# Seven products of quarters for both layers of the last batch in an attention and mixer kernel

## The chip, the cores and the metric

The kernel runs on one core of one Trainium2 chip. A core has five engines with a program each: TensorE (PE in the profile, with its weight loads as PEld), VectorE (DVE), ScalarE (ACT), GpSimd (POOL) and SyncE (SP), which here only starts DMAs. TensorE multiplies a stationary block[...] with a moving block and accumulates into PSUM; VectorE and ScalarE read PSUM and SBUF[...]. The metric is the device time of the whole kernel in microseconds (us); lower is better. Three runs of the kernel before gave 1704.02, 1704.91 and 1705.40 us, median 1704.91.

## The reference

Top-k attention over 8 batches and 8 heads (576 rows, head width 64, the 32 largest scores of a row kept), whose output goes as x (8 x 576 x 512) through a mixer:

```
xt = x.transpose(0, 2, 1)
h = xt @ U @ V
u = x + h.transpose(0, 2, 1)
ch = np.maximum(u @ w_ch1, 0.0) @ w_ch2
return (u + ch).astype(np.float32)
```

The two layers of the last but one line are what the change is about: u (576 x 512) times w_ch1 (512 x 2048), everything negative set to zero, times w_ch2 (2048 x 512), for each batch. All of it is in fp32.

## The kernel before

The attention runs in steps of 128 rows of a pair of heads. For each step VectorE looks for the 32 largest scores, GpSimd and ScalarE make mask and exponential, TensorE multiplies by the values. When the four pairs of heads of a batch are done, `mixed` (line 630) has written u, turned, into the tile uT: its 512 channels lie on 4 blocks of 128 partitions, its 576 rows along the columns.

The two layers of a batch are a generator, `mlp` (line 692), put into the list `fillers` by the last `mixed` of the batch. `fill` (line 793) takes matmuls from it in small portions between the steps of the next batch, so that TensorE has work while VectorE searches. The last batch has no next batch: its generator is emptied by the loop at the end of the kernel. The program order of each engine is the order in which this code emits instructions; nothing reorders it later.

`mlp` takes the columns of uT in two spans, 320 and 256 wide (`SPAN`). In each span:

- layer one: for each of the 16 blocks of 128 hidden channels, 4 matmuls (line 701) with a block of w1 as stationary and a block of uT as moving operand, summed in one PSUM buffer `mm` of two; ScalarE writes its positive part into hT (line 714);
- layer two: for each of the 4 blocks of output channels, 16 matmuls (line 719) with w2 and hT; then u is added (in the last batch by VectorE, line 731, in the others by ScalarE and GpSimd, lines 733 and 734).

One matmul of the code is two records in the profile, since fp32 goes through the array in two instructions.

`turned_back` (line 737) brings a result to row order. It is put off by `later(12, ...)` until 12 more matmuls have been emitted (`tick`). In most batches TensorE transposes it into PSUM (line 764), ScalarE copies it (line 766) and one or two DMAs of SP write it out (line 770). In the last batch VectorE transposes in blocks of 32 x 32 instead (line 746), and 8 or 12 DMAs with short rows put the blocks in place (lines 751 and 756); only the very last result goes by TensorE. The tile `ob`, from which these DMAs read, has two buffers, and so has the result tile `oT`.

w1 is one tile of 128 x 4 x 2048, w2 one of 128 x 16 x 512. The PSUM buffers are three pools of two: `sc` (scores), `tp` (transposes and small products) and `mm` (the two layers).

Of the kernel before, what the change touches and what calls it, by code (L numbers as in the profile page):

```python
# [8 lines left out]
F32 = mybir.dt.float32  # L9
U8 = mybir.dt.uint8  # L10
U32 = mybir.dt.uint32
AF = mybir.ActivationFunctionType
ALU = mybir.AluOpType

TOPK = 32
# [11 lines left out]
def kernel(  # L27
# [28 lines left out]
    nc = tc.nc  # L56
    B, H, S, D = q.shape
    P = 128
    C = H * D
    R = moe_U.shape[1] // 2  # L60
    F = moe_w_ch1.shape[1] // 2
    NF, NC = F // P, C // P
    NT, TAIL = 4, 64
    MAIN = NT * P
    HALF = S // 2
# [10 lines left out]
    BLK = 32  # L76
    HT = 8
# [3 lines left out]
    const = ctx.enter_context(tc.tile_pool(name="const", bufs=1))  # L81
    loads = ctx.enter_context(tc.tile_pool(name="loads", bufs=1))
    attn = ctx.enter_context(tc.tile_pool(name="attn", bufs=2))
    small = ctx.enter_context(tc.tile_pool(name="small", bufs=8))
    mlpp = ctx.enter_context(tc.tile_pool(name="mlpp", bufs=2))
# [8 lines left out]
    OFF = {0: 0, 1: P, NT: 2 * P, 2: 2 * P + TAIL, 3: 3 * P + TAIL}  # L94
# [15 lines left out]
        nc.gpsimd.memset(vts[i], 0.0)  # L110
    for x in xs:
        nc.gpsimd.memset(x[:, NT, :], 0.0)
    w1 = const.tile([P, NC, F], F32, name="w1")
    w2 = const.tile([P, NF, C], F32, name="w2")
    U = const.tile([P, NT + 1, R], F32, name="U")

# [9 lines left out]
    def rows(t):  # L126
        return P if t < NT else TAIL
# [74 lines left out]
    for f in range(0, F, SLAB):  # L202
        for cc in range(NC):
            params.append(
                ([moe_w_ch1[cc * P:(cc + 1) * P, 2 * f:2 * (f + SLAB)]], w1[:, cc, f:f + SLAB])
            )
    for c in range(0, C, P):
        for f in range(0, NF, NT):
# [421 lines left out]
    def mixed(g, wait, lag=0):  # L630

        for _ in range(lag):
            yield
        b, gi = divmod(g, NPAIR)
        if gi == 0:
            uTs[b] = mlpp.tile([P, NC, S], F32, tag="uT", name="uT")
        XT, den = XTs.pop(g), dens[g]
        X = xs[g % 2]
        tp = ps_t.tile([P, NT, P], F32, tag="tp", name="tp")
        for t in range(NT):  # L640
            nc.tensor.transpose(tp[:, t, :], XT[:, cols(t)], ident)  # L641
        X4 = X[:, 0:NT, :].rearrange("p t (h d) -> p t h d", h=2)
        tp4 = tp.rearrange("p t (h d) -> p t h d", h=2)
        den4 = den[:, 0 : 2 * NT].rearrange("p (t h) -> p t h ()", h=2).to_broadcast([P, NT, 2, D])
        nc.scalar.copy(X4, tp4)
        nc.gpsimd.tensor_tensor(X4, X4, den4, ALU.mult)
        for _ in range(wait):
            yield
        pT = ps_t.tile([P, P], F32, tag="tp", name="pT")
        for t in range(NT + 1):  # L650
            i = t % NT * R
            nc.tensor.matmul(  # L652
                pT[i : i + R, :],
                lhsT=U[:, t, :],
                rhs=X[:, t, :],
                start=(t < NT),
                stop=(0 < t),
            )
        Tb = mlpp.tile([P, P], F32, tag="Tb", name="Tb")
        nc.scalar.copy(Tb, pT)  # L660
        yield
        for chunks, (lo, hi) in zip(PARTS, SPAN):
            up = ps_t.tile([P, WIDE], F32, tag="tp", name="up")
            nc.tensor.matmul(up[:, 0 : hi - lo], lhsT=Tb, rhs=V[:, lo:hi], start=True, stop=False)  # L664
            for t in chunks:
                nc.tensor.matmul(  # L666
                    up[:, OFF[t] - lo : OFF[t] - lo + rows(t)],
                    lhsT=X[:, t, :],
                    rhs=ident if t < NT else ident2,
                    is_transpose=True if t < NT else None,  # L670
                    start=False,
                    stop=(t == chunks[-1]),
                )
            nc.scalar.copy(uTs[b][:, gi, lo:hi], up[:, 0 : hi - lo])
            yield
        if gi == NPAIR - 1:
            fillers.append(mlp(b))

    posts, ticks = [], 0

    def later(wait, job):

        posts.append((ticks + wait, job))

    def tick():

        nonlocal ticks
        ticks += 1
        if posts and posts[0][0] <= ticks:
            posts.pop(0)[1]()  # L690

    def mlp(b):

        uT = uTs.pop(b)
        for chunks, (lo, hi) in zip(PARTS, SPAN):
            w = hi - lo
            hTs = []
            for f in range(NF):
                ph = ps_m.tile([P, C], F32, tag="mm", name="mm")
                for cc in range(NC):  # L700
                    nc.tensor.matmul(  # L701
                        ph[:, 0:w],
                        lhsT=w1[:, cc, f * P : (f + 1) * P],
                        rhs=uT[:, cc, lo:hi],
                        start=(cc == 0),
                        stop=(cc == NC - 1),
                    )
                    tick()
                    if cc < NC - 1:
                        yield w / C  # L710
                if f % 2 == 0:
                    hT = mlpp.tile([P, 2, WIDE], F32, tag="hT", name="hT", bufs=HT)
                    hTs += [hT[:, 0], hT[:, 1]]
                nc.scalar.activation(hTs[f][:, 0:w], ph[:, 0:w], AF.Relu)  # L714
                yield w / C
            for c in range(NC):
                po = ps_m.tile([P, C], F32, tag="mm", name="mm")
                for f in range(NF):
                    nc.tensor.matmul(  # L719
                        po[:, 0:w],  # L720
                        lhsT=w2[:, f, c * P : (c + 1) * P],
                        rhs=hTs[f][:, 0:w],
                        start=(f == 0),
                        stop=(f == NF - 1),
                    )
                    tick()
                    if f < NF - 1:
                        yield w / C
                oT = mlpp.tile([P, WIDE], F32, tag="oT", name="oT")
                if b == B - 1:  # L730
                    nc.vector.tensor_tensor(oT[:, 0:w], uT[:, c, lo:hi], po[:, 0:w], ALU.add)  # L731
                else:
                    nc.scalar.copy(oT[:, 0:w], po[:, 0:w])
                    nc.gpsimd.tensor_tensor(oT[:, 0:w], oT[:, 0:w], uT[:, c, lo:hi], ALU.add)
                later(12, turned_back(b, chunks, lo, c, oT))
                yield w / C
    def turned_back(b, chunks, lo, c, oT):


        def run():  # L740
            cs = slice(c * P, (c + 1) * P)
            if b == B - 1 and (lo, c) != (SPAN[1][0], NC - 1):

                w = sum(rows(t) for t in chunks)
                ob = mlpp.tile([P, 3 * P], F32, tag="ob", name="ob", bufs=2)
                nc.vector.transpose(ob[:, 0:w], oT[:, 0:w])
                for a in range(4):
                    cs = slice(c * P + a * BLK, c * P + (a + 1) * BLK)
                    ba = ob[a * BLK : (a + 1) * BLK]
                    for t in chunks[0:2]:  # L750
                        nc.sync.dma_start(
                            out[b, 0:MAIN, cs].rearrange("(m i t) c -> t i m c", i=BLK, t=NT)[t],
                            ba[:, OFF[t] - lo : OFF[t] - lo + P].rearrange("i (m c) -> i m c", c=BLK),
                        )
                    if NT in chunks:
                        nc.sync.dma_start(
                            out[b, MAIN:S, cs].rearrange("(m i) c -> i m c", i=BLK),
                            ba[:, 2 * P : 2 * P + TAIL].rearrange("i (m c) -> i m c", c=BLK),
                        )
                return  # L760
            tp = ps_t.tile([P, 3, P], F32, tag="tp", name="tp")
            for i, t in enumerate(chunks):
                n = rows(t)
                nc.tensor.transpose(tp[0:n, i, :], oT[:, OFF[t] - lo : OFF[t] - lo + n], ident)  # L764
            ob = mlpp.tile([P, 3, P], F32, tag="ob", name="ob", bufs=2)
            nc.scalar.copy(ob[:, 0:2], tp[:, 0:2, :])
            if NT in chunks:
                nc.scalar.copy(ob[0:TAIL, 2], tp[0:TAIL, 2, :])
            t = chunks[0]
            nc.sync.dma_start(  # L770
                out[b, 0:MAIN, cs].rearrange("(p t) c -> p t c", t=NT)[:, t : t + 2, :],
                ob[:, 0:2],
            )
            if NT in chunks:
                nc.sync.dma_start(out[b, MAIN:S, cs], ob[0:TAIL, 2])

        return run

    MLP_WORK = 2 * NF * NC * S / C

# [230 lines left out]
```

## Time and profile before

| | |
|---|---|
| median of three runs | 1704.91 us |
| the profiled execution | 1704.56 us |
| its span, first to last instruction | 1702.7 us |
| mean granted TensorE clock | 0.97 |
| TensorE busy | 1606.2 us, 94% |
| VectorE busy | 1495.9 us, 88% |
| ScalarE busy | 993.5 us, 58% |
| GpSimd busy | 900.5 us, 53% |
| chain that ended last | TensorE 85%, VectorE 12% |

A busy share is an average over the span. A line of the chain gives the share of the span that a line of code holds on the path that ended last: 29% each for the matmuls of line 719 and of line 701. A group line gives line, engine, operation, output and input tiles and shapes, the count, then busy time and the mean of one in ns, then the idle time of the engine just before and what ended it.

From 1574.16 us on, TensorE works on the two layers of the last batch, and from 1580.84 us on nothing else is left of the batches before:

| window, us | TensorE | VectorE | ScalarE | GpSimd |
|---|---|---|---|---|
| 1500 to 1510 | 10.00 | 10.00 | 7.69 | 5.79 |
| 1560 to 1570 | 10.00 | 0.00 | 1.81 | 1.72 |
| 1600 to 1650 | 50.00 | 4.00 | 3.35 | 0.00 |
| 1650 to 1690 | 40.00 | 1.73 | 5.00 | 0.00 |

### The profile page before, as it was taken

The page shows a single profiled execution, that of the slowest core. Times are in us where ns is not written, and L with a number is a line of the kernel's source. Part 1 is how long each engine was busy: PE and PEld are TensorE (multiplying, and loading weights), DVE is VectorE, ACT ScalarE, POOL GpSimd, SP SyncE. Part 2 cuts the span into 40 slices and gives each one's busy share as a digit, 9 for nine tenths or more (in the row PEclk, how much of TensorE's full clock was granted, in tenths as well). Part 3 has the DMA queues.
Part 4 walks back from the last instruction along what each step waited for, and adds up shares of the span by engine and source line. Part 5 has one row for each costly group of instructions (what it writes and reads, how often), then busy time and mean ns, then how long its engine had stood idle before and what let it go on. Part 6 is the DMA issues. An engine that isn't in the chain of part 4 may idle for free.

```text
span 1702.7 us, 29005 instructions
## 1 busy us (share of the span) xinstructions
PE 1606.2 (94%) x9385; PEld 1210.6 (71%) x9385; DVE 1495.9 (88%) x4286; ACT 993.5 (58%) x2422; POOL 900.5 (53%) x695
## 2 busy tenths in 40 slices
PE   4566789999999999999999999999999999999999
PEld 2444556787677877788777877788777877788777
DVE  7999998999999999999999999999999999991000
ACT  4888778665556656565656556565656556563100
POOL 4778568656555555555555555555555555551000
PEclk7788899999999999999999999999999999999999
DMA  3322232255445454554544454554544454532010
GB/s 87 96 83 85 65 85 69 63 135 129 124 122 128 118 134 119 140 127 118 124 123 125 122 130 119 137 127 122 125 122 124 120 135 117 134 106 79 4 16 13
DMA packets 275832, 180.95 MB, mean 106 GB/s; under 512 B 173920, under 2 KB 260192, under 8 KB 275680
## 3 DMA queue, kind: packets, MB, share of 16 engines
q1 hardware_dynamic: 259648, 117.49, 29.8%
q10 hardware_dynamic: 16032, 61.61, 11.3%
q8 instruction: 74, 1.21, 0.3%
q14 instruction: 78, 0.64, 0.1%
HBM read 108.23 MB, written 70.78 MB: 105 GB/s over the span
## 4 chain that ended last, share of the span: by engine, by line
PE 85%; DVE 12%; ACT 1%; POOL 1%; issue 1%; DMA 0%; SPq 0%; DVEq 0%; POOLq 0%; ACTq 0%
PE mm L719 29%; PE mm L701 29%; PE sc L334 9%; PE O L618 7%; DVE m L485 5%; DVE upper L480 5%; PE up L664 2%; PE O L602 2%; DVE first L467 2%; PE O L615 1%; PE tp L577 1%; PE up L666 1%; PE pT L652 1%; PE tp L764 1%; PE tp L641 1%; DVE w L186 1%
## 5 line engine op out<-in xcount | busy, mean ns | idle before, releaser
L719 PE MATMUL mm<-hT,w 128*128 128x256 f32 (+1 forms) x2048 | 530.4, 409 | 0.0
L701 PE MATMUL mm<-uT,w 128*128 128x256 f32 (+1 forms) x2048 | 529.6, 410 | 0.0
L515 POOL TENSOR_TENSOR Ssb<-Ssb,E 128x576 f32<-128x576 f32 x243 | 339.7, 1417 | 275.7 <-ACT E L514 275.4
L701 PEld LDWEIGHTS mm<-uT,w 128*128 128x128 f32 x2048 | 379.2, 191 | 109.5 <-issue 8.4
L719 PEld LDWEIGHTS mm<-hT,w 128*128 128x128 f32 x2048 | 377.2, 190 | 104.4 <-issue 12.7
L485 DVE MAX8 m<-upper 128x8 f32<-128x304 f32 (+1 forms) x780 | 367.2, 512 | 0.7
L480 DVE MATCH_REPLACE8 upper<-m,upper 128x304 f32<-128x304 f32 (+1 forms) x520 | 259.7, 507 | 0.0
L397 POOL TENSOR_TENSOR lower<-Ssb 128x576 uint32<-128x576 uint32 x108 | 152.7, 1414 | 152.8 <-issue 100.1
L334 PE MATMUL sc<-qkT 64*128 64x288 f32 (+1 forms) x1334 | 210.2, 437 | 11.2 <-ACT Ssb L367 7.8
L404 ACT ACTIVATE Ssb<-Ssb,nmax 128x576 f32<-128x576 f32 x258 | 200.9, 780 | 18.6 <-POOL Ssb L491 9.7
L714 ACT ACTIVATE hT<-mm 128x320 f32<-128x320 f32 (+1 forms) x256 | 104.6, 409 | 181.9 <-PE mm L701 178.2
L400 POOL TENSOR_TENSOR lower<-lower,upper 128x576 uint32<-128x576 uint32 x108 | 152.7, 1414 | 100.3 <-DVE upper L399 95.2
L452 DVE MAX8 upper<-lower 128x8 f32<-128x288 f32 x432 | 172.3, 440 | 9.8 <-POOL lower L400 9.7
L514 ACT ACTIVATE E<-Ssb,least 128x576 f32<-128x576 f32 x243 | 176.2, 768 | 4.3
L334 PEld LDWEIGHTS sc<-qkT 64*128 64x128 f32 (+1 forms) x1334 | 115.6, 182 | 73.7 <-issue 29.0
L541 DVE STREAM_TRANSPOSE y<-Ssb 128x512 f32<-128x512 f32 (+1 forms) x312 | 154.8, 546 | 7.0 <-ACT Ssb L404 6.4
L360 ACT COPY Ssb<-sc 128x576 f32<-128x576 f32 x216 | 127.7, 644 | 36.6 <-PE sc L334 36.6
L618 PE MATMUL O<-PT,va 128*64 128x128 f32 x2048 | 144.5, 285 | 0.0
L731 DVE TENSOR_TENSOR oT<-uT,mm 128x320 f32<-128x320 f32 (+1 forms) x8 | 3.6, 454 | 144.6 <-PE mm L719 144.6
L618 PEld LDWEIGHTS O<-PT,va 128*64 128x64 f32 x2048 | 113.1, 140 | 16.1 <-issue 1.3
L399 DVE TENSOR_TENSOR upper<-sc,Ssb 128x576 f32<-128x576 f32 x108 | 80.3, 744 | 22.2 <-ACT Ssb L360 22.0
L480 DVE MATCH_REPLACE8 upper<-first,upper 128x304 f32<-128x304 f32 x216 | 97.7, 460 | 0.0
(111 smaller groups left out, 1893.3 us busy)
## 6 DMA issues: line engine op xcount, KB each, us to landing
away<-y SPq DMA_DIRECT2D x416, 144.0 KB, 2.5
PT<-away ACTq DMA_DIRECT2D x104, 576.0 KB, 3.8
raw<-in_moe_w_ch_dram SPq DMA_DIRECT2D x32, 512.0 KB, 3.8
va<-in_v_dram SPq DMA_DIRECT2D x64, 128.0 KB, 2.3
out_dram<-ob SPq DMA_DIRECT2D x57, 128.0 KB, 2.0
ld<-in_q_dram SPq DMA_DIRECT2D x108, 64.0 KB, 2.7
ld<-in_k_dram SPq DMA_DIRECT2D x108, 64.0 KB, 2.5
ld<-in_q_dram SPq DMA_DIRECT2D x108, 8.0 KB, 3.0
```

The costliest lines, as they stand in the source:

```text
L334: nc.tensor.matmul(out, lhsT=qkT[half(h), 0, cols(t)], rhs=qkT[half(h), 1, lo:hi], start=True, stop=True,)
L397: nc.gpsimd.tensor_tensor(bottom, a.bitcast(U32), b.bitcast(U32), ALU.add)
L404: nc.scalar.activation(E, chunk, AF.Exp, bias=nmax, scale=SCALE, accum_out=total)
L452: nc.vector.max(spot, lower)
L480: nc.vector.match_replace(nxt, ms[c], curs[c], NEG)
L485: nc.vector.max(ms[c], curs[c])
L514: nc.scalar.activation(gap, chunk, AF.Relu, bias=least[:, c : c + 1], scale=-WIDEN)
L515: nc.gpsimd.tensor_tensor(chunk, chunk, gap, ALU.subtract)
L541: nc.vector.transpose(y[:, :, i * NT : i * NT + c].rearrange("p r c j -> p c r j"), E2[:, a : a + c * P].rearrange("p (c r j) -> p c r j", ...
L618: nc.tensor.matmul(O[half(h)], lhsT=va[:, h, j, :], rhs=PT[:, NT * h + j], start=False, stop=(j == NT - 1),)
L701: nc.tensor.matmul(ph[:, 0:w], lhsT=w1[:, cc, f * P : (f + 1) * P], rhs=uT[:, cc, lo:hi], start=(cc == 0), stop=(cc == NC - 1),)
L719: nc.tensor.matmul(po[:, 0:w], lhsT=w2[:, f, c * P : (c + 1) * P], rhs=hTs[f][:, 0:w], start=(f == 0), stop=(f == NF - 1),)
```

## The change

The last batch goes through a new generator, `closing`, in place of `mlp`. It cuts the stationary matrix A, the moving matrix B and the result C of each layer into quarters and computes the four quarters of C with seven products instead of eight:

```
S1 = A21+A22   S2 = S1-A11    S3 = A11-A21   S4 = A12-S2
T1 = B12-B11   T2 = B22-T1    T3 = B22-B12   T4 = B21-T2
P1 = A11 B11   P5 = S1 T1     P6 = S2 T2     P7 = S3 T3
U2 = P1+P6     U3 = U2+P7
C11 = P1 + A12 B21     C12 = U2 + P5 + S4 B22
C21 = U3 + A22 T4      C22 = U3 + P5
```

The columns are cut into 288 and 288. Layer one goes in 8 rounds, each for one block of hidden channels of the lower and one of the upper half, with 2 matmuls in a product; layer two in 2 rounds with 8 matmuls in a product. x, y and z are three accumulators in three pools of PSUM: x collects C11, y collects P5 and then C12, z collects P6, P7 and the last product of C21; P1, P5, U2 and U3 are read from them in between, while the matmuls of other accumulators run. The last product of a round's z (`held`) is put off until two products of the next round have been emitted. The weight sums of layer one are made by GpSimd two rounds ahead, those of layer two by VectorE, into the space of w1, which is cut into four tiles for that (`w1s`). The differences of layer one's results are made by VectorE (`turned_sums`). The results of layer one lie in the tiles that the attention no longer needs. In `give`, all four results of the first round of layer two and the first of the second go by VectorE's transpose and 12 DMAs each; the last three go by TensorE's transpose, put off by 5 matmuls.

```
-    w1 = const.tile([P, NC, F], F32, name="w1")
+    W1Q = F // NT
+    w1s = [const.tile([P, NC, W1Q], F32, name=f"w1{i}") for i in range(NT)]
...
-            fillers.append(mlp(b))
+            fillers.append(closing(b) if b == B - 1 else mlp(b))
...
+    def closing(b):
...
+        def sums(engine, a11, a12, a21, a22, s1, s2, s3, s4):
+            engine.tensor_tensor(s1, a21, a22, add)
+            engine.tensor_tensor(s3, a11, a21, sub)
+            engine.tensor_tensor(s2, s1, a11, sub)
+            engine.tensor_tensor(s4, a12, s2, sub)
...
+        nc.vector.tensor_tensor(t1, b12, b11, sub)
+        nc.vector.tensor_tensor(t2, b22, t1, sub)
+        nc.vector.tensor_tensor(t3, b22, b12, sub)
+        nc.vector.tensor_tensor(t4, b21, t2, sub)
...
+        def first_sums(j):
+            raw_ = mlpp.tile([P, 2 * C], U32, tag="raw", name="raw", bufs=3)
...
+            sums(nc.gpsimd, *weights(j), *blocks_)
...
+        sets = {0: first_sums(0), 1: first_sums(1)}
...
+            def turned_sums(j):
+                h11, h12, h21, h22, x1, x2, x4 = halves[j]
+                nc.vector.tensor_tensor(x1, h12, h11, sub)
+                nc.vector.tensor_tensor(h12, h22, h12, sub)
+                nc.vector.tensor_tensor(x2, h22, x1, sub)
+                nc.vector.tensor_tensor(x4, h21, x2, sub)
...
+            def fourth(j, z, p1, a22):
+                yield from product(z, a22, t4, False)
+                h21 = halves[j][2]
+                nc.vector.tensor_tensor(h21, z, p1, add)
+                nc.scalar.activation(h21, h21, AF.Relu)
...
+            for j in range(KF):
...
+                x = ps_s.tile([P, 2, 512], F32, tag="sc", name="sc")[:, 0, 0:HALF]
+                y = ps_t.tile([P, C], F32, tag="tp", name="tp")[:, 0:HALF]
+                z = ps_m.tile([P, C], F32, tag="mm", name="mm")[:, 0:HALF]
+                p1, p5, u2, u3 = temporaries()
+                yield from product(x, a11, b11)
+                nc.scalar.copy(p1, x)
+                yield from product(y, s1, t1)
+                nc.scalar.copy(p5, y)
+                if held:
+                    nc.scalar.activation(halves[j - 1][3], halves[j - 1][3], AF.Relu)
+                    yield from held
+                if j + 2 < KF:
+                    sets[j + 2] = first_sums(j + 2)
+                yield from product(z, s2, t2)
+                nc.vector.tensor_tensor(u2, z, p1, add)
+                if ahead:
+                    ahead.pop(0)()
+                yield from product(x, a12, b21, False)
+                nc.scalar.activation(h11, x, AF.Relu)
+                yield from product(y, s4, b22, False)
+                nc.vector.tensor_tensor(h12, u2, y, add)
+                nc.scalar.activation(h12, h12, AF.Relu)
+                yield from product(z, s3, t3, False)
+                nc.vector.tensor_tensor(u3, z, p1, add)
+                nc.gpsimd.tensor_tensor(h22, u3, p5, add)
+                if j > 0:
+                    turned_sums(j - 1)
+                held = fourth(j, z, p1, a22)
+                if j == KF // 2:
+                    ahead = s_of(0)
...
+            for m in range(KC):
...
+                yield from product(x, a11, h11s)
+                p1u = attn.tile([P, MAIN], F32, tag="XT", name="XT", bufs=1)[:, 0:HALF]
+                nc.scalar.copy(p1, x)
+                nc.gpsimd.tensor_tensor(p1u, p1, u21, add)
+                if held:
+                    nc.scalar.activation(halves[-1][3], halves[-1][3], AF.Relu)
+                    yield from held
+                    held = None
+                    turned_sums(KF - 1)
+                    ahead = s_of(1)
+                yield from product(y, s1, t1s)
+                nc.scalar.copy(p5, y)
+                nc.gpsimd.tensor_tensor(p5, p5, u22, add)
+                yield from product(z, s2, t2s)
+                nc.vector.tensor_tensor(u2, z, p1, add)
+                nc.gpsimd.tensor_tensor(u2, u2, u12, add)
+                yield from product(x, a12, h21s, False)
+                give(b, m, 0, x, u11, m == 0 or None)
+                yield from product(z, s3, t3s, False)
+                nc.vector.tensor_tensor(u3, z, p1, add)
+                give(b, m + KC, 1, u3, p5, m == 0)
+                yield from product(y, s4, h22s, False)
+                give(b, m, 1, y, u2, m == 0)
+                while ahead:
+                    ahead.pop(0)()
+                yield from product(z, a22, t4s, False)
+                give(b, m + KC, 0, z, p1u, m == 0)
...
+    def give(b, c, n, part, rest, blocks_=True):
+
+        oT = mlpp.tile([P, WIDE], F32, tag="oT", name="oT")
+        nc.vector.tensor_tensor(oT[:, 0:HALF], part, rest, ALU.add)
...
+        if blocks_ is not False:
+            ob = mlpp.tile([P, 3 * P], F32, tag="ob", name="ob", bufs=2)
+            nc.vector.transpose(ob[:, 0:HALF], oT[:, 0:HALF])
+            for a in range(4):
...
+            return
+
+        def run():
+            tp = ps_t.tile([P, 3, P], F32, tag="tp", name="tp")
+            for i in range(2):
+                nc.tensor.transpose(tp[:, i, :], oT[:, at_ + i * P : at_ + (i + 1) * P], ident)
+            nc.tensor.transpose(tp[0:BLK, 2, :], oT[:, tail_at : tail_at + BLK], ident)
+            ob = mlpp.tile([P, 3, P], F32, tag="ob", name="ob", bufs=2)
+            nc.scalar.copy(ob[:, 0:2], tp[:, 0:2, :])
+            nc.scalar.copy(ob[0:BLK, 2], tp[0:BLK, 2, :])
...
+        later(5, run)
```

`s_of(m)` lists the four weight sums of layer two's round m (VectorE, 1024 elements each). `mlp` and `turned_back` lose their branches for the last batch.

## The prediction

> **What bounds the kernel now.** I read the page's slices first, then the chain of waits after 1573 us, then the groups by shape. The slices (tenths of busy time in 40 slices; the last row is the granted TensorE clock):
>
> ```profile
> PE   4566789999999999999999999999999999999999
> ...
> DVE  7999998999999999999999999999999999991000
> ...
> POOL 4778568656555555555555555555555555551000
> PEclk7788899999999999999999999999999999999999
> ```
>
> In the last three slices TensorE is full at full clock and VectorE and GpSimd have almost nothing to do. The chain in order of time (start, length, what) says what fills them:
>
> ```profile
> 1574.16 6.46 PE mm L701 x24
> 1580.62 0.22 PE tp L764 x2
> 1580.84 28.00 PE mm L701 x104
> 1608.84 34.45 PE mm L719 x128
> 1643.29 27.63 PE mm L701 x128
> 1670.92 27.64 PE mm L719 x128
> ...
> 1698.58 0.43 DVE oT L731
> ...
> 1699.06 0.45 PE tp L764 x2
> ```
>
> This is the last batch, alone: 512 records (two for each matmul in the code), 124.18 us, 0.22 us of transposes, not one wait. The span ends 4.14 us after the last matmul (1702.70 - 1698.56). So here every matmul removed is time removed, as long as TensorE isn't made to wait.
>
> **What one record costs.** 320 columns: 34.45 / 128 = 0.2691 us; 256 columns: 27.64 / 128 = 0.2159 us; that is 0.83 ns a column. 288 columns, halfway: 0.2425 us. A busy neighbourhood doesn't change this: 24 records of 256 columns at 1507.89 us took 5.18 us (0.2158 each) while VectorE was busy 10.00 of 10 us and GpSimd 5.79.
>
> **What the change removes and adds on TensorE.** Ahead of the last batch the order on all engines stays as it was. Then, per layer, 7 products of quarters in place of 8: layer one 8 rounds x 7 x 2 matmuls, layer two 2 rounds x 7 x 8, together 224 matmuls or 448 records of 288 columns: 448 x 0.2425 = 108.64 us. The old batch's transposes stay (0.22). In the second round two groups of three output transposes now stand before the last matmul, at 0.11 us each (two took 0.22): 0.66 us. Sum 109.52 against 124.40: **-14.88 us**, if nothing waits.
>
> **Costs beside it.** The rows nearest to the new operations (mean ns after the busy time):
>
> ```profile
> L731 DVE TENSOR_TENSOR oT<-uT,mm 128x320 f32<-128x320 f32 x4 | 2.0, 488 | 93.0 <-PE mm L719 93.0
> L731 DVE TENSOR_TENSOR oT<-uT,mm 128x256 f32<-128x256 f32 x4 | 1.7, 421 | 51.5 <-PE mm L719 51.5
> L734 POOL TENSOR_TENSOR oT<-oT,uT 128x320 f32<-128x320 f32 x28 | 24.2, 865 | 38.5 <-ACT oT L733 38.5
> L734 POOL TENSOR_TENSOR oT<-oT,uT 128x256 f32<-128x256 f32 x28 | 20.4, 730 | 28.8 <-ACT oT L733 28.2
> ```
>
> VectorE: 1.05 ns an element, so 0.455 us for 288 and 1.22 us for the 1024 of a second-layer weight sum. GpSimd: 0.73 us for 256, 0.80 for 288. ScalarE reads 320 in 0.44 and 256 in 0.39 (line 714), so 0.41 for 288.
>
> *Start.* uT is complete at 1568.7 (the copies of line 674), the new products begin at 1574.16. The four input differences (576 elements, 0.75 each, row of line 399: 744 ns) need 3 us. GpSimd is free from 1566.7 and its first eight weight sums need 8 x 0.73 = 5.8 us, to 1572.5. Both hide behind the batch before; without that cover they would cost up to 5.8.
>
> *Layer one, one round* of 14 matmuls lasts 14 x 0.485 = 6.79 us. Its products end at 0.97 (x), 1.94 (y), 2.91 (z of the round before), 3.88 (z), 4.85 (x), 5.82 (y), 6.79 (z). Work per round: VectorE 4 additions from PSUM and 4 turned sums, 8 x 0.455 = 3.64, in three rounds 1.22 more; GpSimd 4 x 0.73 + 0.80 = 3.72; ScalarE six of 0.41 = 2.5. All below 6.79. What matters is each read that must end before the accumulator is written again: x and y are copied 0.4 us after their first product and written 2.9 us later; z is read after 3.88 and written from 5.82; read after 6.79 and written 1.94 later. A read takes 0.46 with its 0.02 and 0.04 us hand-overs (as between lines 719, 731 and 764 at the end), so the tightest has 1.5 us to spare. **Cost on the path: nothing**, unless VectorE comes late.
>
> *VectorE beside GpSimd.* The turned sums read two SBUF tensors each. The Trainium skill speaks against that (SBUF — State Buffer, "Who interferes with whom"): such a VectorE instruction and a GpSimd one that reads SBUF exclude each other, and the second waits for the first to finish. One place of the trace shows the pair:
>
> ```profile
> 191.55 0.81 DVE L494 SCALAR_TENSOR_TENSOR Ssb<-Ssb,m,E 128x576 f32<-128x576 f32 x1
> ...
> 191.71 1.80 POOL L187 TENSOR_TENSOR w<-w,raw 128x512 uint32<-128x512 uint32 x1 [3.54 <-DVE w L186]
> ```
>
> GpSimd came second and took 1.80 instead of its mean 1.31; VectorE, first, took 0.81 (0.77 the other time). So the rule holds here. What does it do to a round? After z's last read (0.48 into the next round) four turned sums stand on VectorE ahead of the next reads, and GpSimd has five operations. In turn, VectorE first: VectorE ends at 0.48 + 4 x 0.455 + (0.80 + 2 x 0.73) = 4.56, then two reads, z free at 5.47, needed at 5.82: no wait. In turn, GpSimd first: one more GpSimd turn, z free at 6.2, 0.4 us of wait; in about five rounds (the last two have no weight sums, the first no turned ones) 2 us. GpSimd always first: VectorE starts at 4.2, z free at 6.95, 1.1 us, five times: 5.7. By the row I take the first, **0**; by the harsh reading of the rule 5.7. Below nothing it can't be.
>
> *Between the layers* the last turned column is ready at about 4.85 + 2 x 0.455 + hand-overs, and read by the eighth matmul of the y product, at 8.2. Nothing.
>
> *Layer two.* A product lasts 8 x 0.485 = 3.88 us. In its first round four results go through VectorE's transpose and 12 output DMAs each, on SP:
>
> ```profile
> L751 SPq DMA_DIRECT2D out_dram<-ob x56: 315/430/2113, 1618.7 to 1695.8; - x56
> ```
>
> With the 0.04 between issues, 12 take 5.7 us, more than 3.88, and there are two ob buffers. Counted from the layer's start: results are ready at 16.5, 20.4, 24.3 and 28.1; SP runs from 17.5 without a pause to about 40; the third transpose waits for the first set to land (24.7), the fourth for the second (30.2). Behind the third transpose on VectorE stand the weight sums of the second round, done from 26.5 to 30; TensorE wants the first at 32.0. So 5.5 us of slack hide the queue. Without it each us of delay would be a us of time. The second round's first result (43.7) finds SP empty, and its 12 DMAs are issued by 50.4, before the outputs at 51, 55 and the end.
>
> *End.* After the last matmul: the addition has 288 columns (+0.03), three transposes (+0.11), and a second copy and DMA behind the first. SP starts it 0.44 later; a small transfer lands in 1.5 us, the large one in 1.8, so it adds 0.14 to 0.44; I take 0.34. **+0.5 us.**
>
> **Sum:** -14.88 + 0.5 = -14.4 us. The profiled execution took 1704.56 us (span 1702.7 and 1.86 around it), so **1690.2 us**, with a span of about 1688.3. The profiled one lies 0.35 below the median of 1704.91; from that it would be 1690.5.
>
> **Rivals.**
> 1. *VectorE and GpSimd hold each other up* and TensorE waits for z in layer one: for it, the two lines above and the full queues; against it, the slack of 1.5 us. 2 to 5.7 us: 1692 to 1696. Chance 0.20.
> 2. *SP's queue sets the end.* Its issues took up to 2.1 us once. If the mean for the 60 blocked DMAs rose from 0.47 to 0.70, they would end at 17.5 + 42 = 59.5, and the six DMAs behind them, 2.6 us, at 62 instead of about 58: +4, 1694. Against it: such issues held 0.43 in the median. Chance 0.07.
> 3. *Slower: TensorE waits at the borders of the products and loses its clock.* There are 70 products in place of 32 long sums. The trace shows the clock following the load: in 0 to 200 us TensorE is busy 60% at clock 0.79, in 200 to 400 us 95% at 0.97. The skill warns of it (TensorE: Matmul & The Clock Gate, "A second HAM failure mode: psum-queue depth-cycling"): changing PSUM banks with small gaps can throw the clock back and forth between half and full. By the rule, a tenth of the stretch at half clock costs 11 us, a quarter 27; by the rows, today's change of buffer after every 8 or 32 records costs nothing. Decisive point: with 92% busy the clock, between those two windows, is about 0.955, so 9.4 us of gaps and 5.1 of clock eat the gain; that is 0.13 us at each border. A whole exposed read, 0.5 us at each of 56 borders, would be 28 us, and the time about 1704.6 + 14 + 15 of clock = 1733. Against it: between a read and the next write of the same accumulator lie always at least 1.9 us of other products. Chance 0.05.
>
> That the change doesn't take effect can't be: 224 matmuls stand where 256 stood.
>
> **Chances and range.** Forecast 0.66, rivals 0.20, 0.07, 0.05, and 0.02 for a loss that just cancels the gain. A difference under 0.2% (3.4 us) can't be told from none. Faster 0.93, same 0.02, slower 0.05. Range: down to 1688.6, if 288 columns take 0.240 each, 1.1 less in all, and a median lies half a microsecond low, as the shown runs spread by 1.4; up to 1695.5, nearly all of rival 1 and 2.
>
> **What would show it.** Right: the new matmuls back to back, 448 records from 1574.2 to about 1683.7, clock 1.00, no waits for z; GpSimd's 256-element sums stretched while VectorE's turned sums run. Wrong: idle TensorE before the third z product with VectorE as releaser (rival 1); the last DMAs issued long after their copies (2); granted clock below 0.96 after 1574 (3).

## The result, and the profile after

The changed kernel takes 1690.03 us (median of four runs, 1689.40 to 1690.71) against 1704.47 us for the kernel before in the same series: ratio 0.9916, 95% interval 0.9904 to 0.9929. That is 14.4 us less. The profiled execution took 1690.17 us, its span is 1688.4 us.

The slices of the changed kernel, in the same rows as before:

```profile
PE   4667799999999999999999999999999999999999
...
DVE  7999998999999999999999999999999999994452
...
POOL 4778668655555555555555555555555555553620
PEclk7787798999999999999999999999999999999999
```

TensorE is full to the end at full clock, as before. New is the work of VectorE and GpSimd in the last three slices. The chain in order of time from 1573 us on (start, length, what):

```profile
1572.86 1.51 PE mm L725 x7
1574.37 0.97 PE sc L801 x4
1575.34 0.97 PE tp L801 x4
1576.31 0.97 PE mm L801 x4
...
1580.19 0.22 PE tp L749 x2
...
1675.47 2.42 PE tp L801 x10
1677.89 0.22 PE tp L1003 x2
1678.11 0.11 PE tp L1004
...
1683.00 2.07 issue
1685.07 0.37 ACT ob L1006
```

Line 801 is the matmul of a product; sc, tp and mm are the pools in which x, y and z lie. A product of layer one takes 0.97 us, and the next begins where it ends. The line "issue" covers the last records, which the chain lost: in the timeline the last product's last two records begin at 1683.24 and take 0.65, so the matmuls end at 1683.89. From the first product to there it is 109.52 us. The only wait of TensorE from 1570 us on, in the list of its waits (who waited for what, us in total, times, longest), comes behind the last matmul:

```profile
PE tp L1003 <- DVE oT L981: 0.5, 1, 0.5
```

I use one measure for all kernels below, free of what the 1574 us ahead vary by from run to run (the batch began between 1572.8 and 1575.2): **from the first matmul of the last batch to the end of the span**, given to 0.1 us, as the spans are. Before: 1702.7 - 1574.16 = 128.5 us. After: 1688.4 - 1574.37 = 114.0 us, 14.5 less. One execution of the kernel with all reads exposed took 4094.89 us, 2.4 times the others; it is left out of that kernel's row below, which rests on three runs, and its profile comes from a second series.

### The profile page after: what moved, and what is told of

Its sections match the earlier page's. It is cut to its first block, busy times and chain, and to the rows that moved or that the text cites. A ratio compares the mean times of both kernels' runs of the same rounds, so it can differ in the third digit from the quotient of the medians.

```text
span 1688.4 us, 29105 instructions
## 1 busy us (share of the span) xinstructions
PE 1597.7 (95%) x9328; PEld 1202.3 (71%) x9328; DVE 1544.0 (91%) x4364; ACT 1001.9 (59%) x2447; POOL 938.1 (56%) x741
## 4 chain that ended last, share of the span: by engine, by line
PE 82%; DVE 14%; ACT 1%; issue 1%; POOL 1%; DMA 1%; SPq 0%; ACTq 0%; DVEq 0%; POOLq 0%
PE mm L725 26%; PE mm L707 24%; PE sc L335 9%; PE O L619 7%; DVE m L486 6%; DVE upper L481 5%; PE mm L801 3%; PE up L665 2%; DVE first L468 2%; PE O L603 2%; PE tp L801 2%; PE sc L801 2%; PE O L616 1%; PE tp L578 1%; PE up L667 1%; PE tp L749 1%
## 5 line engine op out<-in xcount | busy, mean ns | idle before, releaser
L707 PE MATMUL mm<-uT,w 128*128 128x320 f32 (+1 forms) x1792 | 468.7, 412 | 0.3 <-ACT hT L720 0.3
L725 PE MATMUL mm<-hT,w 128*128 128x320 f32 (+1 forms) x1792 | 468.0, 410 | 0.0
L707 PEld LDWEIGHTS mm<-uT,w 128*128 128x128 f32 x1792 | 331.6, 191 | 96.9 <-issue 9.0
L725 PEld LDWEIGHTS mm<-hT,w 128*128 128x128 f32 x1792 | 328.8, 190 | 90.7 <-issue 12.7
L720 ACT ACTIVATE hT<-mm 128x320 f32<-128x320 f32 (+1 forms) x224 | 91.2, 407 | 100.8 <-PE mm L707 96.4
L628 ACT COPY XT<-O 128x128 f32<-128x128 f32 x128 | 33.9, 265 | 107.1 <-PE O L619 106.9
```

The costliest lines, as they stand in the source:

```text
L707: nc.tensor.matmul(ph[:, 0:w], lhsT=first_layer(cc, f), rhs=uT[:, cc, lo:hi], start=(cc == 0), stop=(cc == NC - 1),)
L725: nc.tensor.matmul(po[:, 0:w], lhsT=w2[:, f, c * P : (c + 1) * P], rhs=hTs[f][:, 0:w], start=(f == 0), stop=(f == NF - 1),)
```

## The experiments

The theory: the time of the last batch is the number of its matmuls times their spacing, and all that the change adds lies beside them. The rivals: the gain has another source; the sums or the output queue cost time after all; waits at the product borders, with or without a loss of clock, are what the order with three accumulators avoids.

| kernel | median, us | ratio to before (95%) | last batch to the end, us |
|---|---|---|---|
| before | 1704.2 to 1704.5 | 1 | 128.5 |
| changed | 1690.03 | 0.9916 (0.9904 to 0.9929) | 114.0 |
| one product twice | 1705.48 | 1.0005 (0.9997 to 1.0014) | 129.5 |
| no sums | 1690.23 | 0.9919 (0.9904 to 0.9934) | 114.0 |
| more output buffers | 1690.17 | 0.9917 (0.9903 to 0.9932) | 114.0 |
| short tail | 1690.87 | 0.9924 (0.9908 to 0.9941) | 115.0 |
| last product at once | 1696.55 | 0.9956 (0.9941 to 0.9970) | 120.3 |
| VectorE loaded | 1698.30 | 0.9964 (0.9950 to 0.9978) | 122.1 |
| all reads exposed | 1715.71 | 1.0070 (1.0053 to 1.0087) | 142.4 (second series) |
| changed, second series | 1690.65 | 0.9920 (0.9907 to 0.9934) | 114.0 |
| two queues, second series | 1689.31 | 0.9914 (0.9900 to 0.9927) | 113.5 |

### One product twice

```
                 yield from product(x, a11, b11)
+                yield from product(x, a11, b11)
...
                 yield from product(x, a11, h11s)
+                yield from product(x, a11, h11s)
```

> The first product of every round of both layers is computed twice, so eight products' worth of matmuls with the same sums, reads and buffers; the output doesn't change. Theory (TensorE bounds the last batch and the gain is the number of matmuls): 32 matmuls more at 0.485 us, +15.5 us on 1690.0, so 1705.5 us, about 1 us above the kernel before. Rival (the gain comes from the new layout of columns, accumulators or outputs, not from the count): clearly under 1700 us.

Measured: 1705.48 us, and from the last batch's first matmul to the end 129.5 us. Against 114.0 that is 15.5 us; 64 records of 0.2425 us are 15.52. Here too TensorE's only wait comes behind the last matmul:

```profile
PE tp L1005 <- DVE oT L983: 0.6, 1, 0.6
```

The kernel is as slow as the one before, with all the rest of the change in it. So the gain is the eighth product, and nothing else about the new generator shows a gain.

### No sums

```
-            sums(nc.gpsimd, *weights(j), *blocks_)
-            return [pieces(x) for x in blocks_]
+            return [pieces(x) for x in weights(j)]
...
-                nc.vector.tensor_tensor(x1, h12, h11, sub)
-                nc.vector.tensor_tensor(h12, h22, h12, sub)
-                nc.vector.tensor_tensor(x2, h22, x1, sub)
-                nc.vector.tensor_tensor(x4, h21, x2, sub)
+                halves[j] = [h11, h12, h21, h22, h11, h12, h21]
```

and in the same way for the input differences and the weight sums of layer two.

> Leaves out all weight sums, input differences and turned sums; the products take the plain quarters in their place, so the output is not the reference's. TensorE's program is the same. Theory (the sums are hidden): 1690.0 us within 0.4. Rival (VectorE and GpSimd hold each other up and TensorE pays): 1 to 5 us less.

Measured: 1690.23 us; 114.0 us in the last batch, as with the sums. In the 66 us from 1574 us VectorE's busy time falls from 38.7 to 14.6 us and GpSimd's from 28.7 to 8.6, and the time stays. The sums cost no time that shows. The excerpt of the timeline of the changed kernel's third round, which begins at 1587.20, shows that they do get in each other's way (start, length, engine, line; VectorE first, then GpSimd, each in its own order):

```profile
1588.16 0.87 DVE L884 TENSOR_TENSOR hT<-hT 128x288 f32<-128x288 f32 x1
1588.95 0.98 DVE L885 TENSOR_TENSOR hT<-hT 128x288 f32<-128x288 f32 x1
1590.04 0.80 DVE L886 TENSOR_TENSOR hT<-hT 128x288 f32<-128x288 f32 x1
...
1591.22 0.46 DVE L920 TENSOR_TENSOR PTt<-mm,upper 128x288 f32<-128x288 f32 x1
```

```profile
1588.68 0.94 POOL L794 TENSOR_TENSOR raw<-w 128x256 f32<-128x256 f32 x1
1589.58 0.94 POOL L795 TENSOR_TENSOR raw<-w,w 128x256 f32<-128x256 f32 x1
1590.48 0.94 POOL L796 TENSOR_TENSOR raw<-raw,w 128x256 f32<-128x256 f32 x1
1591.50 0.73 POOL L797 TENSOR_TENSOR raw<-w,raw 128x256 f32<-128x256 f32 x1
```

Alone, a turned sum takes 0.45 us (line 883, just ahead of these) and a weight sum 0.73. Side by side they take up to 0.98 and 0.94. GpSimd's sums follow each other every 0.90 us, less than the 1.18 that one of each would take in turn. So the two engines hold each other up, but not for whole instructions. The rounds without weight sums are the check: in the eighth, line 885 is back at 0.45 us, while line 884, beside GpSimd's addition of line 930 (1621.78 to 1622.66), is stretched as before:

```profile
1622.11 0.86 DVE L884 TENSOR_TENSOR qkT<-qkT 128x288 f32<-128x288 f32 x1
1622.90 0.45 DVE L885 TENSOR_TENSOR PT<-qkT 128x288 f32<-128x288 f32 x1
```

In the third round VectorE's read that sets z free (line 920) ends at 1591.68, 4.48 us into the round; the third z product begins at 5.82. That leaves 1.34 us, and the next experiment uses it up.

### VectorE loaded

```
-                nc.vector.tensor_tensor(x1, h12, h11, sub)
+                for _ in range(5):
+                    nc.vector.tensor_tensor(x1, h12, h11, sub)
```

> The first turned sum of each round is made five times instead of once: four more VectorE instructions of 0.455 us with two SBUF inputs, same output. In the changed kernel z is free 4.5 us into a round and needed at 5.82, so 1.3 us of slack. Theory: 4 x 0.455 plus some blocking by GpSimd exceed it by about 1.1 us in the four rounds in which GpSimd makes weight sums, and by nothing in the others: +4.6 us, 1694.6 us, with TensorE waiting for VectorE's read of z. Rival (VectorE is far from mattering): 1690 us.

Measured: 1698.30 us, the last batch 8.0 us longer. TensorE's waits in it (those behind the last matmul left out here and below):

```profile
PE mm L801 <- DVE PTt L921: 5.3, 4, 1.3
PE tp L801 <- DVE y L884: 1.1, 1, 1.1
```

The waits are where the theory had them: for the read of z by VectorE (line 921 here), four times 1.33 us, in the rounds with weight sums, and in no other round of layer one. One was not foreseen: at the start of layer two the last turned sums come 1.1 us late. Together 6.4 us, where 4.6 were expected, and still 1.6 less than the batch grew. The next kernel shows the rest.

### The last product at once

In layer one `held` is not put off:

```
-                    yield from held
...
                 nc.gpsimd.tensor_tensor(h22, u3, p5, add)
+                yield from fourth(j, z, p1, a22)
```

> Only the putting off of a round's last product is undone in layer one: its read of z is exposed once in a round. Theory: 8 x 0.52 = +4.2 us, 1694.2 us, clock 1.00. Rival (clock follows the busy share): 93% busy, clock about 0.96 in layer one, +2 us more, 1696.5 us. Rival (the read is hidden anyway): 1690 us.

Measured: 1696.55 us, the last batch 6.3 us longer. The number is the rival's; its mechanism is not there, since the granted clock in the stretch is 1.00. TensorE's waits, and the chain around one read of z:

```profile
PE mm L801 <- DVE PTt L928: 4.2, 8, 0.6
...
1587.62 0.98 PE mm L801 x4
1588.62 0.47 DVE PTt L928
1589.14 1.24 PE mm L801 x4
1590.37 0.97 PE sc L801 x4
```

The eight waits take 0.52 us on average: 0.55 at seven places, and 0.33 at the first, where transposes of the batch before fill part of the gap. But the product behind the wait also takes 1.24 us instead of 0.97. In the timeline of this place the weight load waited too (the bracket: idle time before it, and for whom):

```profile
1587.45 1.13 PE L801 MATMUL mm<-Stail,raw 128*128 128x288 f32 x4
1588.62 0.46 DVE L928 TENSOR_TENSOR PTt<-mm,upper 128x288 f32<-128x288 f32 x1 [0.52 <-PE mm L801]
1589.13 0.78 PEld L801 LDWEIGHTS mm<-lower,w 128*128 128x128 f32 x4 [1.01 <-DVE PTt L928]
1589.14 1.24 PE L801 MATMUL mm<-lower,w 128*128 128x288 f32 x4 [0.55 <-DVE PTt L928]
```

The starts alone give the price of a stop. The four records from 1587.45 on begin 0.2425 us apart, the last at 1588.18; the first behind the stop begins at 1589.14, 0.96 later, and the second another 0.35 later. In a stream both steps take 0.2425, so the stop costs 0.71 + 0.10 = 0.82 us, 0.27 more than the idle time of 0.55:

- 0.164 us: a record is shown with 406 ns, and the next begins 242 ns after it, so that in a stream the rest is covered. VectorE's read does begin only 0.44 us after the start of the last record.
- 0.104 us: the weight load of the first record begins with it (1589.13 and 1589.14), where in the stream it begins 0.24 earlier. That this is the reason for the late second record fits the times, but no run tests it alone.

The Trainium skill (TensorE: Matmul & The Clock Gate, "Single matmul latency") gives a single bf16 matmul at full clock 398 cycles of 2.4 GHz beside one for each column. With two cycles a column, which the spacing of 242 ns for 288 columns suggests, that makes an estimate of (398 + 576) / 2.4 = 406 ns, the length of the records here. It is no test of the page, as the profile models the ends of its matmuls.

So 4.2 + 8 x 0.27 = 6.3 us, as measured. The same term completes the loaded kernel: its five gaps are 6.46 us of idle time (the brackets: 4 x 1.33 and 1.14), and with 5 x 0.27 that is 7.8 of 8.0. The rest stands in its last two rounds of layer one, where the third z product begins without an idle gap, but its second record comes 0.10 us late each time.

### All reads exposed

In layer one, each accumulator is filled to its end before the next:

```
                 yield from product(x, a11, b11)
                 nc.scalar.copy(p1, x)
+                yield from product(x, a12, b21, False)
+                nc.scalar.activation(h11, x, AF.Relu)
                 yield from product(y, s1, t1)
                 nc.scalar.copy(p5, y)
...
-                    yield from held
...
+                yield from product(y, s4, b22, False)
                 yield from product(z, s2, t2)
...
-                yield from product(x, a12, b21, False)
-                nc.scalar.activation(h11, x, AF.Relu)
-                yield from product(y, s4, b22, False)
...
                 yield from product(z, s3, t3, False)
...
+                yield from fourth(j, z, p1, a22)
```

> In layer one each accumulator is filled to its end before the next: x, x, y, y, z, z, z. So all four reads of a round stand between two products of the same accumulator. Theory with a clock that doesn't react to gaps of half a microsecond: 8 rounds x (2 x 0.46 by ScalarE + 2 x 0.52 by VectorE) = +15.7 us, 1705.7 us at clock 1.00: about the whole gain. Rival (the clock follows the busy share, as in the third rival of the prediction): TensorE 78% busy in layer one, clock about 0.88 there, +7 us more, 1713 us.

The three runs gave 1715.35 to 1717.44 us, slower than before the change, and no profile of their own. By these three runs the +26.5 us of the text that follows is 25.7:

> The kernel with all reads exposed once more, for a profile. The runs gave +26.5 us where 15.7 were expected. After a wait for one read the other experiment shows 0.51 us of idle time and 0.27 us by which the next product takes longer. Theory now: each of 32 exposed reads costs 0.82 us, 26.2 in all, TensorE's granted clock stays at 1.00. Rival: clock below 0.95 in layer one.

Measured the second time: 1717.81 us, ratio 1.0080 (1.0061 to 1.0098), the last batch 28.3 us longer. TensorE's waits, and the first 66 us of layer one (window, then busy us of TensorE, its weight loads, VectorE, ScalarE and GpSimd, granted clock, DMA):

```profile
PE mm L801 <- DVE PTt L922: 5.2, 8, 0.7
PE mm L801 <- DVE PTt L928: 4.4, 8, 0.6
PE sc L801 <- ACT upper L911: 4.2, 8, 0.5
PE tp L801 <- ACT upper L915: 4.0, 7, 0.6
PE tp L801 <- POOL raw L797: 0.6, 1, 0.6
```

```profile
1574.00:1640.00 66.00, 51.32 (x187) 32.86 (x186) 25.49 (x45) 16.57 (x41) 23.40 (x32) 1.00 0.01 4
```

32 waits, 18.4 us, 0.58 each (at one of them GpSimd's weight sum came later than the read). With 0.27 for each restart that makes 27.0 us; up to the last matmul the batch is 26.7 us longer, 0.83 for each stop. The other 1.6 us lie behind the last matmul, in a part that the edit doesn't touch: SP's last DMA issue took 2.10 us there, and 0.42 in the changed kernel. TensorE is busy 78% of the stretch and its granted clock is 1.00: gaps of half a microsecond did not cost clock here. So interleaving x, y and z, and putting off the last product, is worth about 26 us (25.7 by the medians of the first series), nearly twice the gain. Without it the change would lose: these medians lie 11.5 and 13.5 us above the kernel before.

### More output buffers

```
+            if n == 0:
+                ob = attn.tile([P, S], F32, tag="E", name="E")
+            else:
                 ob = mlpp.tile([P, 3 * P], F32, tag="ob", name="ob", bufs=2)
```

> Every other block-wise output uses another free tile, so VectorE's two waits for output DMAs (0.58 and 1.12 us) go. Theory (hidden by the 5 us of slack before the second round's weight sums are wanted): 1690.0 us within 0.4. Rival (the SP queue sets the end of the second round): 1 to 2 us less.

Measured: 1690.17 us, the last batch 114.0 us. In the changed kernel the two waits are there, in the timeline's brackets:

```profile
1653.33 0.48 DVE L986 STREAM_TRANSPOSE ob<-oT 128x288 f32<-128x288 f32 x1 [0.58 <-DMA out_dram<-ob]
...
1659.93 0.48 DVE L986 STREAM_TRANSPOSE ob<-oT 128x288 f32<-128x288 f32 x1 [1.12 <-DMA out_dram<-ob]
```

In the experiment they are gone, and nothing follows. The first weight sum of the second round, which stands behind the first of these waits, ends at 1654.91; the product that needs it begins at 1659.95.

### Short tail, and two queues

The short tail sends one more result (the sixth of eight, so the third from the end) by VectorE's transpose and 12 DMAs, and has ScalarE start the small last DMAs:

```
-                give(b, m + KC, 1, u3, p5, m == 0)
+                give(b, m + KC, 1, u3, p5)
...
-            nc.sync.dma_start(out[b, MAIN + n * BLK : MAIN + (n + 1) * BLK, cs], ob[0:BLK, 2])
+            nc.scalar.dma_start(out[b, MAIN + n * BLK : MAIN + (n + 1) * BLK, cs], ob[0:BLK, 2])
```

> The sixth result from the end goes by VectorE's transpose and 12 DMAs instead of three TensorE transposes, and the small output DMAs of the last results are started by ScalarE instead of by SP behind the large one. Theory: -0.33 us of transposes and -0.2 to -0.3 us at the end, 1689.4 us. Rival (the 12 further DMAs on SP run late): the last DMA is issued later than 1.6 us after the last matmul and the time doesn't fall or rises by up to 1 us.

Measured: 1690.87 us, the last batch 1.0 us longer in the trace; by the times the intervals of the two kernels overlap. The last large DMA is issued late, as the rival said. From the end of its timeline (issues of SP and of ScalarE, and the last copy with what it waited for):

```profile
1678.13 1.94 SPq L991 DMA_DIRECT2D out_dram<-ob  x2
...
1684.36 0.43 SPq L995 DMA_DIRECT2D out_dram<-ob  x1
1684.89 1.94 SPq L1008 DMA_DIRECT2D out_dram<-ob  x2
1686.04 0.37 ACT L1006 COPY ob<-tp 128x256 f32<-128x256 f32 x1 [3.48 <-DMA out_dram<-ob]
1686.59 0.33 ACTq L1012 DMA_DIRECT2D out_dram<-ob  x1
```

The 12 further DMAs keep SP busy to 1684.79, 1.3 us beyond the last product. The last copy stood ready after the transposes at about 1684.6, but its buffer was still in use by those DMAs; it starts at 1686.04. TensorE's 0.33 us were saved and about 1.3 us lost behind them. Part of that is chance: one of the two issues at 1678.13 took 1.47 us, where the others took 0.43, and everything behind it came 1.04 later. The changed kernel has such an issue too (1.67 us, at 1647.26), where the slack hides it. So the trace shows how a DMA queue near the end reaches the end, but not that it always costs 1 us.

Two queues takes queue and buffer away as a cause, both at once: half of the blocks' DMAs go to ScalarE's queue, the further buffers of the experiment before are added, and then all results but the last go by VectorE's transpose. The small last DMA is again ScalarE's.

```
+                queue = nc.sync if a % 2 == 0 else nc.scalar
...
-                        nc.sync.dma_start(
+                        queue.dma_start(
...
-                give(b, m, 1, y, u2, m == 0)
+                give(b, m, 1, y, u2)
```

> The changed kernel itself, beside which the next one is read: 1690.0 us.

> All results of layer two but the last go by VectorE's transpose; their 12 DMAs each are shared by the queues of SP and ScalarE, every other tile lies in further buffers, and the last small DMA is started by ScalarE. Theory (TensorE's 0.66 us of transposes and 0.2 to 0.3 us behind the last matmul are all that is left to take in the last batch outside the products; the queue of SP alone was what made the short tail lose): 0.9 us less than the changed kernel, 1689.1 us. Rival (ScalarE's DMA issues hold up its copies of the accumulators and TensorE waits): 1690 us or more.

Measured: 1689.31 us beside 1690.65 for the changed kernel in the same series, last batch 113.5 against 114.0. The matmuls end 108.87 us after they began instead of 109.52: the 0.66 us of transposes are gone. The end behind them is no shorter (4.65 us; 4.51 in the changed kernel): the large last DMA took 2.1 us to land instead of 1.9, and the last landing comes 3.6 us after the matmuls in both. By the trace it is the fastest of all, by 0.5 us. By the times the intervals against before (0.9900 to 0.9927 and 0.9907 to 0.9934) overlap, so a gain over the changed kernel isn't shown by them. Which of the two, queue or buffer, held up the short tail was not tested apart.

## Why the prediction was right

The forecast was 1690.2 us; the median is 1690.03. By its steps:

- **Matmuls.** Predicted 109.52 us from the first product to the end of the last; the timeline has 109.52. The spacing of 288 columns, taken as halfway between two measured ones, holds to the last digit shown. One product twice confirms the price from the other side: 15.5 us for 64 records.
- **Beside it nothing.** Confirmed by no waits of TensorE before the last matmul, and by the kernel without sums.
- **Start.** It is hidden, as predicted, with less room than predicted: three of the four input differences ran beside GpSimd's weight sums and took 1.3 us each instead of 0.75, and GpSimd was done at 1574.13 instead of 1572.5. The first product that reads a weight sum begins at 1575.34, and its set was done at 1569.73.
- **VectorE beside GpSimd.** The value taken, no wait, was right; the sum to it was too dear. Predicted were VectorE's turned sums ending 4.56 us into a round and z free at 5.47; measured are 3.64 and 4.48. The prediction let every pair take turns for whole instructions (2.26 us in all); the three sums that were stretched lost 0.42, 0.53 and 0.35, 1.3 us. The rule is seen in both engines' stretched lengths, its "waits for the first to finish" only in part. The row of the prediction showed that already: GpSimd began 0.65 us before VectorE ended and took only 0.49 longer than its mean. And the two meet in four rounds, not in about five: the first two have no turned sums beside them.
- **The output queue.** Predicted: SP from 17.5 to about 40 us after the start of layer two (1627.94), waits at the third and fourth transpose, 5.5 us of slack. Measured: 17.5 to 41.6, waits of 0.58 and 1.12 us, 5.0 us. In the short tail this queue does reach the end, when 12 DMAs are put nearer to it: that was the second rival's mechanism, at another place.
- **The end.** Predicted 4.14 + 0.5 us behind the last matmul; measured 4.51. The term was 0.13 too large.
- **What the prediction left open.** The batch began 0.21 us later than in the profile of before; the runs spread by more.

The sum of the errors is 0.1 us in the last batch (-14.5 against -14.4). That the median came within 0.2 us of the forecast is in part luck, as single runs of the changed kernel differ by 1.3 us.

The third rival was mis-sized in both its terms, which the result didn't test but the experiments did. Its price of a border, 0.5 us of wait, leaves out 0.27 us for restarting TensorE. And its loss of clock, drawn from the start of the kernel where a low clock and a low load stand together, doesn't occur in 66 us at 78% load with half-microsecond gaps. So its 1733 us for 56 exposed borders rests on two terms that the runs don't bear out: 32 stops cost 26.7 us, 0.83 each, and no clock. (Its "32 long sums" are layer one alone; with layer two the last batch had 40.)

## What to carry to other kernels

Where one engine works without a wait, take the spacing from its own records and count instructions: here that gave 109.52 us to the digit. Work that frees this engine must be laid beside it with room: each time it stopped for another engine's read, it paid the wait and some more for the restart, here 0.55 and 0.27 us. And before moving more onto a queue that is "hidden", work out when it runs empty: SP's 12 issues for a result, 0.47 us each, were free with 5 us of slack and saved nothing that shows when 12 more ended 1.3 us after the last product.

## What the runs showed of the hardware

- A stop of TensorE for a read cost 0.82 us with 0.55 of idle time in the profile: 0.16 more for the part of a record that the next one covers in a stream, 0.10 for a second record that came late.
- Two tensor operations, on VectorE with both inputs in SBUF and on GpSimd, stretch each other (0.45 to 0.98 us and 0.73 to 0.94 us), but overlap by about 0.28 us per pair: 0.90 us where 0.45 + 0.73 = 1.18.
- The granted clock stayed at 1.00 for 66 us with TensorE 78% busy, in gaps of 0.5 to 0.65 us.
- Single DMA issues of SP take far longer than the median of 0.43 us: in the changed kernel's profile 21 of 1229 took more than 1.2 us. One that is the last of the kernel goes straight into its time (2.10 us instead of 0.42).
